# Load order, weight tiles and ReLU engines in a two-stage attention kernel with an MLP behind it

## The chip, the cores and the metric

One core of one Trainium2 chip runs the kernel. The metric is device microseconds of one execution.

## The reference

For 8 batches, 8 heads, 576 rows and head size 64, two softmax attentions follow one another, and an MLP with squared ReLU works on the result:

```python
def sm_attn(qq, kk, vv):
    s = scale * np.matmul(qq, kk.transpose(0, 1, 3, 2))
    s = s - np.max(s, axis=-1, keepdims=True)
    a = np.exp(s)
    a = a / (np.sum(a, axis=-1, keepdims=True) + 1e-09)
    return np.matmul(a, vv)
p_packed = sm_attn(p, k, v)            # p: 32 rows a head
attn = sm_attn(q, p_packed, p_packed)
x = attn.transpose(0, 2, 1, 3).reshape(4608, 512)
h = x @ w_in                           # 512 x 2048
r = np.maximum(h, 0.0)
out = (s * (r * r) + b) @ w_out        # 2048 x 512; s, b: one number each
```

Inputs and output are float32; the kernel computes in bf16 and accumulates in float32.

## The kernel before, in words

The unit of work is a batch (576 tokens). All matmuls are in one order written out by hand, as are the instructions of the other engines (`mm`, `tr` and the class `Pinned` keep program order, so L71, L74 and L82 are the lines of nearly every record). Steps of a batch `b`:

- `load` (line 93): q, k and v come by DMA issued on POOL, which also casts them to bf16; each has one buffer, so batch b+1's k waits for the last reader of batch b's. `load_p`, `load_w_in` (four chunks of 512 columns) and `load_w_out` (four chunks) use the same queue.
- `prep_p`, `prep_k`, `prep_q` (lines 194 to 254): transposes on PE, copies out of PSUM on DVE and ACT. From batch 3 on (`N_PE_T = 3`), `dma_k` and `dma_q` (lines 221, 256) transpose k and q by DMA from SP's queue instead, `dma_q` from a reordered copy that `order_q` makes on DVE; `order_v` makes another for v.
- `first_scores`, `packed`, `second_scores`, `weights` (lines 262 to 372): the two attentions, with exp on ACT, and ln and exp on ACT in place of a division; `weights` ends with the product `aT` on DVE.
- `packed_w` or `packed_w1` (lines 374, 399): the packed values times W_in, giving the batch's own weights `pw`; `packed_w1` does one chunk of 512 columns, with one half evicted by ACT and the other by DVE.
- `mlp_in(b, m)` (line 430), m from 0 to 15: four matmuls into a PSUM accumulator, a ReLU on ACT to `rlu` (three buffers), a square on DVE into `gT`.
- `Out.step` (line 471): the output tiles of 128 rows, each of 16 accumulating matmuls (steps) with `w_out_sb`; behind the last step DVE adds the bias row and SP stores the tile. `outs(b)` (line 498) gives four tiles for an even batch and five for an odd one; `run_outs(todo, n)` does n steps of them.
- `bias_part` (line 449): the sum of W_out's rows, once, in 16 matmuls.

PSUM holds three accumulators of two banks (pool `psh`, from `big()`) for everything but the output tiles, which have two of one bank (`psy`). `idle(n)` (line 167) is n matmuls on zeros.

The order: the loads are queued as batch 0, two chunks of W_in, batch 1, two chunks of W_in, W_out, p of batches 2 to 7. Lines 522 to 583 are a hand-made list: batch 0's attention, then its MLP inputs mixed with batch 1's attention, then the bias sum with the first output tile of batch 0 and MLP inputs of both batches. From line 585 on a loop over b runs the sixteen `mlp_in(b, m)`; between them stand the output steps of batch b-1 and, by `at(m, ...)`, the attention steps of batch a = b+1 and the loads and transposes of batch c = b+2.

Of the kernel before, what the change touches and what calls it, by code (L numbers as in the profile page):

```python
# [14 lines left out]
def kernel(  # L15
# [25 lines left out]
    P = 128  # L41
# [28 lines left out]
    def mm(*a, **kw):  # L70
        return tc.keep_in_program_order(nc.tensor.matmul(*a, **kw))  # L71
# [68 lines left out]
    bvec = constp.tile([P, 1], F32, name="bvec")  # L140
    sp.dma_start(out=bvec[:], in_=moe_b[0:1].unsqueeze(0).to_broadcast([P, 1]))
    nc.scalar.preload_act_table_set("natural_log_exp_and_others")
    load_w_in(0)
    load_w_in(1)

    KW = H * HS + 32
    kT = [constp.tile([P, KW], BF16, name=f"kT{i}") for i in range(2)]
# [46 lines left out]
    def prep_p(b):  # L194
        i = b % 2
        pt = big(BF16)
        for qd in range(NQ):
            tr(pt[:, 0, qd * P:(qd + 1) * P], pn[:, b, qd, :, :], identb[:])
        for c2 in range(2):
            vec.tensor_copy(  # L200
                out=pbd[i][D * c2:D * c2 + D, :, :, c2, :],
                in_=pt[D * c2:D * c2 + D, 0, 0:NQ * P].rearrange("p (q g j) -> p q g j", q=NQ, g=4),
            )

    def prep_k(b, half):

        i = b % 2
        tp = big(BF16)
        for h4 in range(4):
            for cp in range(CP):  # L210
                tr(
                    tp[:, h4 // 2, (h4 % 2) * HS + cp * R:(h4 % 2) * HS + (cp + 1) * R],
                    kn[b][:, 4 * half + h4, cp * P:(cp + 1) * P],
                    identb[0:R, 0:R],
                )
        vec.tensor_copy(
            out=kT[i][:, half * 4 * HS:(half + 1) * 4 * HS].rearrange("p (a s) -> p a s", a=2),
            in_=tp[:, :, 0:2 * HS],
        )
# [176 lines left out]
            else:  # L396
                vec.tensor_scalar_mul(out=dst, in0=tiles[qd][:], scalar1=rd[b][:, qd:qd + 1])

    def packed_w1(b, ch):

        i = b % 2
        if ch == 0:
            pw[b] = ppw.tile([P, NQ, DFF], BF16, tag="pw", name="pw")
        t = big()
        for qd in range(NQ):
            for pr in range(2):
                hp = 2 * qd + pr
                mm(
                    t[64 * pr:64 * pr + 64, qd, :],
                    ppbd[i][:, hp, :],  # L410
                    w_in_sb[:, hp, ch * NB:(ch + 1) * NB],
                    start=True,
                    stop=True,
                    tile_position=(0, 64 * pr),
                )
        dst = pw[b][:, :, ch * NB:(ch + 1) * NB]
        act.activation(out=dst[:, 0], in_=t[:, 0, :], func=AF.Copy, scale=rd[b][:, 0:1])
        vec.tensor_scalar_mul(out=dst[:, 1], in0=t[:, 1, :], scalar1=rd[b][:, 1:2])


# [6 lines left out]

        return 0 if (b % 4) in (1, 2) else NT * P

    def mlp_in(b, m):  # L430
        hps = big()
        for qd in range(NQ):
            for hf in range(2):
                mm(
                    hps[:, hf, 0:HS],
                    pw[b][:, qd, m * P:(m + 1) * P],
                    aT[b][:, qd, hf * HS:(hf + 1) * HS],
                    start=(qd == 0),
                    stop=(qd == NQ - 1),
                )  # L440
        rlu = ysp.tile([P, 2, HS], BF16, tag="rlu", name="rlu")
        act.activation(out=rlu[:], in_=hps[:, :, 0:HS], func=AF.Relu)
        g0 = slot(b) * S
        vec.tensor_tensor(
            out=gT[:, m, g0:g0 + S].rearrange("p (a s) -> p a s", a=2),
            in0=rlu[:], in1=rlu[:], op=ALU.mult,
        )

    def bias_part(cps, m):
        mm(cps[:], onesb[:], w_out_sb[:, m, :], start=(m == 0), stop=(m == NFF - 1))  # L450
        if m == NFF - 1:
            vec.tensor_scalar_mul(out=biasrep[:], in0=cps[:], scalar1=bvec[:])
# [63 lines left out]

    def loads(b):
        load(kn, k, b, "kn")
        load(vn, v, b, "vn")
        load(qn, q, b, "qn")  # L520

    idle(12)
    twice_p(0, 2)
    prep_k(0, 0)
    prep_p(0)
    first_scores(0, 0)
    prep_k(0, 1)
    first_scores(0, 1)
    prep_p(1)
    packed(0, 0)  # L530
    packed(0, 1)
    idle(3)
    prep_q(0, 0)
    prep_q(0, 1)
    second_scores(0)
    packed_w1(0, 0)
    weights(0, 0)
    weights(0, 1)
    packed_w1(0, 1)
    for m in range(0, 4):  # L540
        mlp_in(0, m)
    prep_k(1, 0)
    mlp_in(0, 4)
    prep_k(1, 1)
    first_scores(1, 0)
    mlp_in(0, 5)
    first_scores(1, 1)
    mlp_in(0, 6)
    packed(1, 0)
    packed(1, 1)  # L550
    mlp_in(0, 7)
    prep_q(1, 0)
    prep_q(1, 1)
    packed_w1(1, 0)
    second_scores(1)
    packed_w1(1, 1)
    weights(1, 0)
    packed_w1(0, 2)
    weights(1, 1)
    mlp_in(0, 8)  # L560
    mlp_in(0, 9)
    packed_w1(1, 2)
    mlp_in(0, 10)
    mlp_in(0, 11)
    packed_w1(0, 3)
    mlp_in(1, 0)
    mlp_in(1, 1)
    packed_w1(1, 3)
    mlp_in(0, 12)
    mlp_in(0, 13)  # L570
    loads(2)
    cps = psy.tile([P, NB], F32, tag="y", name="yps")
    todo = outs(0)
    rest = [(0, 14), (0, 15)] + [(1, m) for m in range(2, 7)]
    for m0 in range(0, NFF, 4):
        for m in range(m0, m0 + 4):
            bias_part(cps, m)
        for x in rest[0:1]:
            mlp_in(*x)
        run_outs(todo, 4)  # L580
        for x in rest[1:2]:
            mlp_in(*x)
        rest = rest[2:]

    for b in range(1, B):
        a = b + 1
        c = a + 1
        steps = {}

        def at(m, *fs):  # L590
            steps.setdefault(m, []).extend(fs)

        if b == 1:
            at(7, lambda: (twice_p(2, B), prep_p(2)))
            at(8, lambda: prep_k(2, 0))
            at(9, lambda: (prep_k(2, 1), first_scores(2, 0)))
            at(10, lambda: first_scores(2, 1))
            at(11, lambda: packed(2, 0))
            at(12, lambda: (packed(2, 1), prep_q(2, 0)))
            at(13, lambda: (prep_q(2, 1), packed_w(2, 0)))  # L600
            at(14, lambda: second_scores(2))
            at(15, lambda: weights(2, 0), lambda: weights(2, 1), lambda: packed_w(2, 1))
            at(10, lambda: loads(3))
            at(15, lambda: dma_k(3))
        elif a < B:
            d = 3 if b == 2 else 0
            at(0 + d, lambda: first_scores(a, 0))
            at(1 + d, lambda: first_scores(a, 1))
            at(3 + d, lambda: packed(a, 0))
            at(4 + d, lambda: packed(a, 1))  # L610
            at(6 + d, lambda: second_scores(a))
            at(8 + d, lambda: packed_w(a, 0))
            at(9 + d, lambda: weights(a, 0))
            at(10 + d, lambda: weights(a, 1))
            at(12 + d, lambda: packed_w(a, 1))
            if b == 2:
                at(1, lambda: (order_q(3), dma_q(3)))
                at(2, lambda: (prep_p(3), order_v(3)))
            if c < B:
                at(4, lambda: loads(c))  # L620
                at(13, lambda: (order_q(c), dma_k(c), dma_q(c)))
                at(15, lambda: (prep_p(c), order_v(c)))
        if b > 1:
            todo = outs(b - 1)
        per = 6 if b == 1 else len(todo)
        if b == 2:
            run_outs(todo, 8)
        for m in range(7 if b == 1 else 0, NFF):
# [9 lines left out]
_INS = ['q', 'k', 'v', 'p', 'moe_w_in', 'moe_w_out', 'moe_s', 'moe_b']  # L638
_OUTS = [((4608, 512), 'float32')]
# [25 lines left out]
```

## Time and profile before

| | |
|---|---|
| median of 3 runs | 286.64 us (286.24 to 288.02) |
| the profiled execution | 287.35 us, of which span 285.6 us |
| mean granted TensorE clock | 0.96 |
| PE busy | 259.3 us (91% of the span) |
| ACT, DVE, POOL busy | 145.8, 144.3, 27.7 us |
| DMA | 34.28 MB, mean 120 GB/s |

PE is the matmul engine (PEld its weight loads), DVE the vector engine, ACT the scalar engine, POOL GpSimd, SP the engine that issues stores and transposes. A record names output and inputs by the program's tile names: `yps` are output steps, `hps<-aT,pw` the matmuls of `mlp_in`, `hps<-w_in_sb,ppbd` those of `packed_w`. A granted clock of 1.00 is 2.4 GHz, 0.50 is 1.2 GHz. Matmuls are pipelined: a group's length holds a drain that the next group covers.

### The profile page before, as it was taken

The numbers are of one execution on the slowest core, as the hardware profiler recorded it, in microseconds if no ns is written. First come the engines' busy times: TensorE is split into PE (matmuls) and PEld (weight loads), VectorE is DVE, ScalarE is ACT, GpSimd is POOL, SyncE is SP. The second block draws the span as 40 slices with busy tenths as digits, with TensorE's granted clock in tenths as the row PEclk, the third lists the DMA queues.
The fourth block names the chain that finished last, engine by engine and source line by source line (L and its number), as shares of the span: only waits on it lengthen the run. The fifth ranks groups of instructions, "written<-read, shape, count | busy, mean of one in ns | idle before, by whom it ended". The sixth has DMA issues, their size and how long they took to land.

```text
span 285.6 us, 5198 instructions
## 1 busy us (share of the span) xinstructions
PE 259.3 (91%) x2127; PEld 145.7 (51%) x2127; DVE 144.3 (51%) x290; ACT 145.8 (51%) x219; POOL 27.7 (10%) x40
## 2 busy tenths in 40 slices
PE   8687869978999969889998999799989999999993
PEld 3544625545545634446555655465556555555441
DVE  3335567363548343735575447645674466444221
ACT  1257698424475434844765466346844674544000
POOL 8163200001201200030003000120000000000000
PEclk9757999999999988979999999999999999999998
DMA  7999999517495994799149951999192211121222
GB/s 86 193 205 205 206 204 198 83 37 115 71 192 80 151 197 82 140 159 221 45 81 154 223 109 37 171 166 204 35 182 67 55 39 38 54 59 37 73 73 73
DMA packets 54567, 34.28 MB, mean 120 GB/s; under 512 B 27408, under 2 KB 49936, under 8 KB 54544
## 3 DMA queue, kind: packets, MB, share of 16 engines
q0 software_dynamic: 25136, 18.61, 45.0%
q1 hardware_dynamic: 29408, 15.34, 25.6%
q8 instruction: 16, 0.26, 0.4%
q14 instruction: 7, 0.06, 0.1%
HBM read 37.23 MB, written 9.44 MB: 163 GB/s over the span
## 4 chain that ended last, share of the span: by engine, by line
PE 74%; DMA 10%; ACT 8%; DVE 5%; issue 1%; POOL 1%; POOLq 0%; DVEq 0%; ACTq 0%
PE yps L71 41%; PE hps L71 31%; DMA qT<-qr 5%; ACT rlu L82 3%; DMA vn<-in_v_dram 3%; DMA kT<-kn 2%; PE hps L74 2%; ACT rcd L82 1%; ACT ld L82 1%; ACT pw L82 1%; DVE gT L82 1%; DVE aT L82 1%; DVE kT L82 1%; DVE qr L82 1%; DVE pw L82 1%
## 5 line engine op out<-in xcount | busy, mean ns | idle before, releaser
L71 PE MATMUL yps<-w_out_sb,gT 128*128 128x512 bf16 x576 | 144.0, 383 | 0.0
L82 ACT ACTIVATE rlu<-hps 128x576 bf16<-128x576 f32 x128 | 82.8, 650 | 91.2 <-PE hps L71 84.3
L82 DVE TENSOR_TENSOR gT<-rlu 128x576 bf16<-128x576 bf16 x128 | 58.4, 457 | 94.2 <-ACT rlu L82 94.0
L71 PE MATMUL hps<-aT,pw 128*128 128x288 bf16 x512 | 85.1, 291 | 3.8 <-DVE aT L82 1.7
L71 PEld LDWEIGHTS <-gT 128*128 128x128 bf16 x576 | 53.2, 98 | 52.5 <-issue 7.5
L71 PEld LDWEIGHTS <-pw 128*128 128x128 bf16 x512 | 50.4, 100 | 41.0 <-issue 5.6
L82 DVE SCALAR_TENSOR_TENSOR ysb<-yps,svec,biasrep 128x512 f32<-128x512 f32 x36 | 26.9, 747 | 15.9 <-PE yps L71 15.8
L82 DVE TENSOR_SCALAR pw<-hps,rd 128x1024 bf16<-128x1024 f32 (+1 forms) x20 | 21.3, 1066 | 4.6 <-ACT pw L82 4.4
L82 ACT ACTIVATE e<-hps 96x768 bf16<-96x768 f32 x16 | 12.9, 804 | 16.4 <-PE hps L71 16.4
L82 POOL DMA_DIRECT2D kn<-in_k_dram x9 | 7.2, 799 | 130.9 <-DMA kT<-kn 84.3
L71 PE MATMUL hps<-w_in_sb,ppbd 128*64 128x512 bf16 x128 | 18.3, 392 | 1.7 <-ACT rlu L82 0.8
L82 ACT ACTIVATE pw<-hps,rd 128x1024 bf16<-128x1024 f32 (+1 forms) x20 | 18.8, 942 | 0.5 <-PE hps L71 0.3
L71 PE MATMUL hps<-pbd,kT 128*128 128x64 bf16 x192 | 9.3, 200 | 9.6 <-DVE pbd L82 3.4
L71 PEld LDWEIGHTS <-ppbd 128*64 128x64 bf16 x192 | 10.0, 113 | 14.0 <-issue 10.4
L82 DVE TENSOR_TENSOR aT<-e,rcd 128x576 bf16<-128x576 bf16 x16 | 12.1, 758 | 9.3 <-ACT rcd L82 9.2
L71 PEld LDWEIGHTS <-kT 128*128 128x128 bf16 x192 | 7.9, 102 | 12.2 <-DMA kT<-kn 4.3
L82 ACT ACTIVATE e<-hps,rs 128x576 bf16<-128x576 f32 x16 | 11.1, 740 | 2.8 <-PE hps L71 2.8
L82 ACT ACTIVATE rcd<-ld 128x576 f32<-128x576 f32 x16 | 10.9, 682 | 0.5
L82 ACT ACTIVATE ld<-hps 128x576 f32<-128x576 f32 x16 | 10.3, 642 | 0.0
L71 PE MATMUL hps<-qT,ppbd 128*64 128x288 bf16 x64 | 7.4, 328 | 2.8 <-DMA qT<-qr 2.3
L82 POOL DMA_DIRECT2D vn<-in_v_dram x8 | 6.2, 775 | 17.4 <-PE hps L71 13.8
L71 PE MATMUL hps<-zeros 128*128 128x512 bf16 x15 | 6.7, 629 | 1.3 <-DVE zeros L82 1.3
(46 smaller groups left out, 115.2 us busy)
## 6 DMA issues: line engine op xcount, KB each, us to landing
vn<-in_v_dram POOLq DMA_DIRECT2D x8, 576.0 KB, 11.2
qn<-in_q_dram POOLq DMA_DIRECT2D x8, 576.0 KB, 13.9
out_dram<-ysb SPq DMA_DIRECT2D x24, 192.0 KB, 2.8
kn<-in_k_dram POOLq DMA_DIRECT2D x7, 576.0 KB, 8.4
out_dram<-ysb SPq DMA_DIRECT2D x24, 128.0 KB, 2.4
w_in_sb<-in_moe_w_in_dram POOLq DMA_DIRECT2D x4, 512.0 KB, 14.3
w_out_sb<-in_moe_w_out_dram POOLq DMA_DIRECT2D x4, 512.0 KB, 20.0
out_dram<-ysb SPq DMA_DIRECT2D x24, 64.0 KB, 2.0
```

What stands on the lines that cost most here:

```text
L71: return tc.keep_in_program_order(nc.tensor.matmul(*a, **kw))
L74: return tc.keep_in_program_order(nc.tensor.transpose(*a, **kw))
L82: return lambda *a, **kw: tc.keep_in_program_order(f(*a, **kw))
```

## The change

All of W_in and W_out is queued behind batch 0 and ahead of batch 1. `mlp_in` and `packed_w1` get a switch `on_act`: with False, `mlp_in` does its ReLU on DVE and its square on POOL, and `packed_w1` evicts both halves on DVE. `m1` uses it for every third `mlp_in` of batches 0 and 1 (m = 2, 5, 8, 11, 14). The list is rewritten: batch 0 is carried through all its MLP inputs, the bias sum (now in an accumulator of `psh`) and two output tiles before batch 1's attention; the other two tiles (32 steps) stand between batch 1's attention steps; batch 1's sixteen `mlp_in` stand with batch 2's attention, and the loop starts with batch 2. Idle matmuls go from 15 to 30. In the loop, the loads, transposes and reorderings of batch c come at other steps, and q is loaded before v from batch 3 on.

```diff
     nc.scalar.preload_act_table_set("natural_log_exp_and_others")
-    load_w_in(0)
-    load_w_in(1)
+    for ch in range(NCH):
+        load_w_in(ch)
+    for m in range(0, NFF, 4):
+        load_w_out(m, m + 4)
...
     load(qn, q, 1, "qn")
-    load_w_in(2)
-    load_w_in(3)
-    for m in range(0, NFF, 4):
-        load_w_out(m, m + 4)
     load_p(2, B)
...
-        act.activation(out=dst[:, 0], in_=t[:, 0, :], func=AF.Copy, scale=rd[b][:, 0:1])
+        if on_act:
+            act.activation(out=dst[:, 0], in_=t[:, 0, :], func=AF.Copy, scale=rd[b][:, 0:1])
+        else:
+            vec.tensor_scalar_mul(out=dst[:, 0], in0=t[:, 0, :], scalar1=rd[b][:, 0:1])
...
-        act.activation(out=rlu[:], in_=hps[:, :, 0:HS], func=AF.Relu)
+        if on_act:
+            act.activation(out=rlu[:], in_=hps[:, :, 0:HS], func=AF.Relu)
+        else:
+            vec.tensor_scalar_max(out=rlu[:], in0=hps[:, :, 0:HS], scalar1=0.0)
         g0 = slot(b) * S
-        vec.tensor_tensor(
+        (vec if on_act else pool).tensor_tensor(
...
-        load(vn, v, b, "vn")
+        if b < N_PE_T:
+            load(vn, v, b, "vn")
         load(qn, q, b, "qn")
+        if b >= N_PE_T:
+            load(vn, v, b, "vn")
+
+    def m1(b, *ms):
+        for m in ms:
+            mlp_in(b, m, on_act=(m % 3 != 2))
```

The new list, in place of lines 522 to 583:

```python
idle(12); twice_p(0, 2)
prep_k(0, 0); prep_p(0); prep_k(0, 1); idle(3)
first_scores(0, 0); first_scores(0, 1); prep_p(1); idle(2)
packed(0, 0); packed(0, 1); idle(5)
prep_q(0, 0); prep_q(0, 1); idle(3)
second_scores(0); packed_w1(0, 0, on_act=False); idle(2)
weights(0, 0); weights(0, 1); idle(3)
packed_w1(0, 1, on_act=False); m1(0, 0, 1, 2, 3, 4)
packed_w1(0, 2, on_act=False); m1(0, 5, 6, 7, 8)
packed_w1(0, 3, on_act=False); m1(0, 9, 10, 11)
todo = outs(0); first, second = todo[0], todo[1]; bps = big()
for m0 in range(0, NFF, 4):
    for m in range(m0, m0 + 4):
        bias_part(bps[:, 0, :], m)
    if m0 < 8:
        m1(0, 12 + m0 // 2)
    first.step(4)
    if m0 < 8:
        m1(0, 13 + m0 // 2)
    second.step(4)
todo = todo[2:]
prep_k(1, 0); prep_k(1, 1); fill(4)      # fill(n): run_outs(todo, n)
first_scores(1, 0); fill(4); first_scores(1, 1); fill(4)
packed(1, 0); packed(1, 1); fill(4)
prep_q(1, 0); prep_q(1, 1); twice_p(2, B); fill(4)
packed_w1(1, 0); second_scores(1); fill(3)
packed_w1(1, 1); weights(1, 0); fill(3)
weights(1, 1); prep_p(2); fill(3)
packed_w1(1, 2); fill(3); loads(2); m1(1, 0, 1)
packed_w1(1, 3); m1(1, 2); prep_k(2, 0); m1(1, 3); prep_k(2, 1)
m1(1, 4, 5); first_scores(2, 0); m1(1, 6); first_scores(2, 1)
m1(1, 7, 8); packed(2, 0); m1(1, 9); packed(2, 1); m1(1, 10, 11)
prep_q(2, 0); prep_q(2, 1); m1(1, 12, 13); loads(3)
second_scores(2); m1(1, 14, 15); packed_w1(2, 0)
todo = outs(1); fill(6); weights(2, 0); fill(3)
packed_w1(2, 1); weights(2, 1); fill(6)
packed_w1(2, 2); fill(3); dma_k(3)
```

And the loop:

```diff
-    for b in range(1, B):
+    for b in range(2, B):
...
-        elif a < B:
-            d = 3 if b == 2 else 0
+        d = 3 if b == 2 else 0
+        if b == 2:
+            at(1, lambda: (packed_w1(2, 3), order_q(3), dma_q(3)))
+            at(2, lambda: (prep_p(3), order_v(3)))
+        if a < B:
             at(0 + d, lambda: first_scores(a, 0))
...
-            if c < B:
-                at(4, lambda: loads(c))
-                at(13, lambda: (order_q(c), dma_k(c), dma_q(c)))
-                at(15, lambda: (prep_p(c), order_v(c)))
+        if c < B:
+            at(1 + d, lambda: loads(c))
+            at(8 + d, lambda: dma_k(c))
+            at(10 + d, lambda: (order_q(c), dma_q(c)))
+            at(12 + d, lambda: order_v(c))
+            at(14, lambda: prep_p(c))
...
-        per = 6 if b == 1 else len(todo)
-        if b == 2:
-            run_outs(todo, 8)
-        for m in range(7 if b == 1 else 0, NFF):
+        per = len(todo)
+        for m in range(NFF):
             mlp_in(b, m)
```

## Rows read from the trace of the kernel before

**Rows 1.** Windows: PE, PEld, DVE, ACT, POOL busy (count), granted clock, DMA share, GB/s

```profile
27.50:48.00 20.50, 16.56 (x242) 10.31 (x240) 13.87 (x28) 17.11 (x29) 2.95 (x4) 1.00 1.33 203
...
92.00:110.00 18.00, 15.64 (x134) 9.01 (x135) 6.25 (x14) 7.32 (x12) 1.53 (x2) 0.91 1.25 173
...
118.00:127.00 9.00, 6.75 (x54) 3.58 (x52) 6.11 (x11) 4.45 (x7) 2.30 (x3) 0.81 1.00 159
...
150.00:153.00 3.00, 2.28 (x24) 1.25 (x22) 2.51 (x5) 1.59 (x3) 0.61 (x1) 1.00 0.97 135
...
180.00:186.00 6.00, 4.08 (x37) 2.44 (x36) 3.31 (x7) 2.11 (x3) 1.21 (x2) 1.00 1.06 177
...
213.00:285.60 72.60, 67.84 (x422) 36.23 (x420) 29.24 (x55) 26.85 (x41) 0.00 (x0) 0.98 0.23 59
```

**Rows 2.** PE's waits: who waited for whom, total us, times, longest

```profile
PE hps L71 <- DMA qT<-qr: 2.3, 1, 2.3
PE hps L71 <- DVE pbd L82: 2.2, 2, 1.7
...
PE hps L71 <- DMA kT<-kn: 1.9, 1, 1.9
```

**Rows 3.** Windows of two us, same columns

```profile
10.00:12.00 2.00, 1.10 (x16) 0.84 (x18) 0.85 (x3) 0.72 (x1) 0.66 (x1) 0.52 1.30 198
...
106.00:108.00 2.00, 2.00 (x12) 0.71 (x9) 0.00 (x0) 1.37 (x2) 0.00 (x0) 0.50 1.19 277
```

**Rows 4.** Timeline of PE: start, length, operation, count [idle before, releaser]

```profile
24.18 3.31 PE L71 MATMUL hps<-aT,pw 128*128 128x288 bf16 x14 [0.85 <-DVE aT L82]
...
85.86 0.87 PE L71 MATMUL hps<-aT,pw 128*128 128x288 bf16 x4
...
92.03 0.51 PE L71 MATMUL hps<-pbd,kT 128*128 128x64 bf16 x12 [0.47 <-DVE pbd L82]
...
106.74 2.31 PE L71 MATMUL yps<-w_out_sb,gT 128*128 128x512 bf16 x5
...
122.95 1.90 PE L71 MATMUL yps<-w_out_sb,gT 128*128 128x512 bf16 x4
```

**Rows 5.** Chain of waits (start, us, what), and one group of 27.5 to 48.0

```profile
46.14 1.71 PE hps L71 x12
...
49.20 0.86 PE yps L71 x4
50.55 0.86 PE yps L71 x4
...
L71 PE MATMUL hps<-aT,pw 128*128 128x288 bf16 x48 | 7.4, 287 | 1.4 <-ACT pw L82 0.9 <-DVE pw L82 0.5
```

**Rows 6.** Groups by form: busy us, mean ns | idle before, releasers

```profile
L82 ACT ACTIVATE rlu<-hps 128x576 bf16<-128x576 f32 x128 | 82.8, 650 | 91.2 <-PE hps L71 84.3 <-DVE rs L82 4.3 <-DVE rd L82 2.4
L82 DVE TENSOR_TENSOR gT<-rlu 128x576 bf16<-128x576 bf16 x128 | 58.4, 457 | 94.2 <-ACT rlu L82 94.0
...
L82 DVE TENSOR_SCALAR pw<-hps,rd 128x512 bf16<-128x512 f32 x8 | 6.0, 749 | 4.6 <-ACT pw L82 4.4
```

**Rows 7.** Timeline of the first 35 us: POOL's work and issues, one weight load

```profile
3.60 0.31 POOL L82 TENSOR_SCALAR_AFFINE_SELECT identb<-identb 128x128 bf16<-128x128 bf16 x1
...
21.09 0.11 PEld L71 LDWEIGHTS <-ppbd 128*64 128x64 bf16 x1 [0.59 <-DMA w_in_sb<-in_moe_w_in_dram]
...
24.15 0.75 POOL L82 DMA_DIRECT2D w_out_sb<-in_moe_w_out_dram  x1 [1.96 <-DMA kn<-in_k_dram]
...
30.27 0.78 POOL L82 DMA_DIRECT2D kn<-in_k_dram  x1 [2.14 <-DMA qn<-in_q_dram]
```

**Rows 8.** Timeline of SP's queue

```profile
122.42 1.41 SPq L82 DMA_DIRECT2D out_dram<-ysb  x2
```

**Rows 9.** Tiles kT and qT: DMA issue to landing, first kT's, then qT's

```profile
DMA to landing us min/median/max: 5.0/5.2/5.4
...
DMA to landing us min/median/max: 4.9/8.0/15.0
```

More of the change, by code (lines that the diff above doesn't have):

```diff
@@ L397, in packed_w, with packed_w1 @@
                 vec.tensor_scalar_mul(out=dst, in0=tiles[qd][:], scalar1=rd[b][:, qd:qd + 1])
-    def packed_w1(b, ch):
+    def packed_w1(b, ch, on_act=True):
         i = b % 2
@@ L428, in tail, with mlp_in @@
         return 0 if (b % 4) in (1, 2) else NT * P
-    def mlp_in(b, m):
+    def mlp_in(b, m, on_act=True):
         hps = big()
@@ L449, in bias_part @@
     def bias_part(cps, m):
-        mm(cps[:], onesb[:], w_out_sb[:, m, :], start=(m == 0), stop=(m == NFF - 1))
+        mm(cps, onesb[:], w_out_sb[:, m, :], start=(m == 0), stop=(m == NFF - 1))
         if m == NFF - 1:
-            vec.tensor_scalar_mul(out=biasrep[:], in0=cps[:], scalar1=bvec[:])
+            vec.tensor_scalar_mul(out=biasrep[:], in0=cps, scalar1=bvec[:])
     def store(ysb, i0, b, col, n):
@@ L525 @@
     prep_p(0)
+    prep_k(0, 1)
+    idle(3)
     first_scores(0, 0)
-    prep_k(0, 1)
     first_scores(0, 1)
     prep_p(1)
+    idle(2)
     packed(0, 0)
     packed(0, 1)
-    idle(3)
+    idle(5)
     prep_q(0, 0)
     prep_q(0, 1)
+    idle(3)
     second_scores(0)
-    packed_w1(0, 0)
+    packed_w1(0, 0, on_act=False)
+    idle(2)
     weights(0, 0)
     weights(0, 1)
-    packed_w1(0, 1)
-    for m in range(0, 4):
-        mlp_in(0, m)
+    idle(3)
+    packed_w1(0, 1, on_act=False)
+    m1(0, 0, 1, 2, 3, 4)
@@ new lines, with fill @@
+    packed_w1(0, 2, on_act=False)
+    m1(0, 5, 6, 7, 8)
+    packed_w1(0, 3, on_act=False)
+    m1(0, 9, 10, 11)
+    todo = outs(0)
+    first, second = todo[0], todo[1]
+    bps = big()
+    for m0 in range(0, NFF, 4):
+        for m in range(m0, m0 + 4):
+            bias_part(bps[:, 0, :], m)
[6 more added lines that the diff above has]
+    todo = todo[2:]
+    def fill(n):
+        run_outs(todo, n)
@@ L542 @@
     prep_k(1, 0)
-    mlp_in(0, 4)
     prep_k(1, 1)
+    fill(4)
     first_scores(1, 0)
-    mlp_in(0, 5)
+    fill(4)
     first_scores(1, 1)
-    mlp_in(0, 6)
+    fill(4)
     packed(1, 0)
     packed(1, 1)
-    mlp_in(0, 7)
+    fill(4)
     prep_q(1, 0)
     prep_q(1, 1)
+    twice_p(2, B)
+    fill(4)
     packed_w1(1, 0)
     second_scores(1)
+    fill(3)
     packed_w1(1, 1)
     weights(1, 0)
-    packed_w1(0, 2)
+    fill(3)
     weights(1, 1)
-    mlp_in(0, 8)
-    mlp_in(0, 9)
+    prep_p(2)
@@ L562 @@
+    fill(3)
     packed_w1(1, 2)
[L563 to L567, printed above, removed]
-    packed_w1(1, 3)
[L569 to L583, printed above, removed]
@@ L585 @@
-    for b in range(1, B):
+    fill(3)
+    loads(2)
+    m1(1, 0, 1)
+    packed_w1(1, 3)
+    m1(1, 2)
+    prep_k(2, 0)
+    m1(1, 3)
+    prep_k(2, 1)
+    m1(1, 4, 5)
+    first_scores(2, 0)
+    m1(1, 6)
+    first_scores(2, 1)
+    m1(1, 7, 8)
+    packed(2, 0)
+    m1(1, 9)
+    packed(2, 1)
+    m1(1, 10, 11)
+    prep_q(2, 0)
+    prep_q(2, 1)
+    m1(1, 12, 13)
+    loads(3)
+    second_scores(2)
+    m1(1, 14, 15)
+    packed_w1(2, 0)
+    todo = outs(1)
+    fill(6)
+    weights(2, 0)
@@ L586 @@
+    fill(3)
+    packed_w1(2, 1)
+    weights(2, 1)
+    fill(6)
+    packed_w1(2, 2)
+    fill(3)
+    dma_k(3)
+    for b in range(2, B):
         a = b + 1
@@ L591, in at @@
             steps.setdefault(m, []).extend(fs)
[L593 to L604, printed above, removed]
-        elif a < B:
-            d = 3 if b == 2 else 0
+        d = 3 if b == 2 else 0
[3 more added lines that the diff above has]
+        if a < B:
             at(0 + d, lambda: first_scores(a, 0))
@@ L615 @@
             at(12 + d, lambda: packed_w(a, 1))
-            if b == 2:
-                at(1, lambda: (order_q(3), dma_q(3)))
-                at(2, lambda: (prep_p(3), order_v(3)))
-            if c < B:
-                at(4, lambda: loads(c))
-                at(13, lambda: (order_q(c), dma_k(c), dma_q(c)))
-                at(15, lambda: (prep_p(c), order_v(c)))
-        if b > 1:
+        if c < B:
[4 more added lines that the diff above has]
+            at(14, lambda: prep_p(c))
+        if b > 2:
             todo = outs(b - 1)
-        per = 6 if b == 1 else len(todo)
-        if b == 2:
-            run_outs(todo, 8)
-        for m in range(7 if b == 1 else 0, NFF):
+        per = len(todo)
+        for m in range(NFF):
             mlp_in(b, m)
@@ L631 @@
                 f()
-            run_outs(todo, per)
-        run_outs(todo, NFF * (NT + 1))
+            fill(per)
+        fill(NFF * (NT + 1))
     todo = outs(B - 1)
     while todo:
-        run_outs(todo, NFF)
+        fill(NFF)
 _INS = ['q', 'k', 'v', 'p', 'moe_w_in', 'moe_w_out', 'moe_s', 'moe_b']
```

## The prediction

> **What bounds the kernel now.** I read the windows by stage first, then PE's waits with their releasers, then fine windows for the clock, and last the rows of single engines and queues. In the windows [rows 1] the reader is to see three regimes. From 27.5 to 48.0 us PE is busy 16.56 of 20.5: batch 1's attention steps and batch 0's MLP inputs run with no output tiles between them, and ACT (17.11) and DVE (13.87) empty accumulators about as fast as PE fills them. Late in the kernel PE is full: 67.84 of the last 72.60, the rest being the tail after the last matmul. Between lie holes: 2.36 us in 92 to 110, 2.25 in 118 to 127, 0.72 in 150 to 153 and the same again in 210 to 213, 1.92 in 180 to 186. Their releasers are the transposed queries, pbd's copies waiting in a full DVE queue, and kT arriving late [rows 2]. Behind the first two holes PE also runs at 1.2 GHz for a while: the granted clock is 0.50 in 106 to 108 [rows 3], five output steps took 2.31 us and, behind the second, four took 1.90 [rows 4], where 0.215 each and a drain of 0.17 make 1.24 and 1.03. That is some 1.2 us beyond each of the two.
>
> **The sum** is made against the profiled execution (287.35 us; span 285.6, so 1.75 outside it), which lies 0.71 above the median 286.64 of the runs; a saving is taken off either. PE's prices at 2.4 GHz: four output steps are 0.86 us in a period of 1.35 that also holds one mlp_in, so an output step is 0.215 and an mlp_in 0.49 [rows 5]. Twelve matmuls in 1.71 us hold a packed_w1 and two mlp_in; without those and the drain a packed_w1 is 0.55 [rows 5]. A batch's attention steps: 16.56 less the twelve mlp_in there (48 matmuls [rows 5]) and six packed_w1 leaves 7.4, of which I take off 1.4 for eleven drains that the next group covers: 6.0. Other engines [rows 6]: ReLU on ACT 0.65, square on DVE 0.457, half of a packed_w1 on DVE 0.749. The ReLU on DVE has no row; 576 columns for 512 make 0.84 of the last, between 0.65 (ACT's) and twice that.
>
> **1. The loads.** W_in 2 and 3 and W_out move ahead of batch 1 on POOL's queue. W_in 1 landed when its matmul was released, at 21.05 us; POOL's sixteenth issue was held until 24.15, when the eighth (batch 1's k) landed, the eighteenth until 30.27, when the tenth landed [rows 7]. So at most eight are under way, they land in order, and 576 KB take 3.07 us, 512 KB 2.73. Forward from 21.05: W_in 2 23.8, W_in 3 26.5, W_out 29.3 to 37.4, batch 1's k 40.5, v 43.6, q 46.6. POOL is held until the ninth lands (26.5) and then issues p, so its first square begins at 27.5.
>
> **2. Start to the first mlp_in.** It hangs on the landings of v, q and W_in 0, which stay. The change adds fifteen idle matmuls, 3.9 us at 2.4 GHz, in waits for those landings. If they keep the clock up (before, it fell to 0.52 in 10 to 12, with PE busy 1.10 of 2 us [rows 3]), second scores end 1 us earlier and the chain of exp, ln, exp and product brings the first mlp_in at 23.2 instead of 24.2 [rows 4]: plus 1.0. If not, the idles cost 7.7 us at 1.2 GHz, of which about 3 fall behind the landings: minus 2.
>
> **3. First mlp_in to batch 2's loop.** Batch 0's first twelve mlp_in with three packed_w1, both halves now on DVE: 6 x 0.749, 4 ReLUs x 0.84, 8 squares x 0.457 = 11.5 us on DVE against 7.0 on PE. PE is let on when the third accumulator from the end is empty: 10.6 us, to 33.9. Bias sum and two output tiles: 48 x 0.215 + 4 x 0.49 = 12.3, to 46.1; the last W_out is wanted at 43.5 and q of batch 1 at 53, each some 6 us after landing, so the new order of the loads costs nothing. Batch 1's attention with 32 output steps: 6.0 + 6.9 + 3 x 0.55 + 0.15 for prep_p = 14.7; walking the list with three accumulators adds 1.8, mostly ACT's exp, ln, exp. 16.5, to 62.6. Then batch 1's sixteen mlp_in with batch 2's attention, and no output step between them, since batch 1's tiles need the last square: 7.8 + 0.55 + 5.5 = 13.9 on PE; the walk adds 3.7, to 80.2 (at the 81% that PE was busy from 27.5 to 48.0 it would be 17.2 for my 17.6). Three packed_w1, weights and 18 steps: 6.0 + 0.4, to 86.6. Bounds: with no wait 80.7, with all waits doubled 92. Before, the loop began at 85.9 [rows 4] with eight output steps done instead of 18 and one packed_w1 more: 10 x 0.215 - 0.55 = 1.6, so 87.4 for the same work. **The start gains about 0.8 (bounds +6.7 and -5).**
>
> Squares on POOL (ten): POOL has no two-input row. Bounds 0.46 (DVE's own) and 2.8 (twice 576/128 of the affine select's 0.313 [rows 7]); I take the single 1.4. Its buffer is wanted again three mlp_in later, 1.7 us at least, so nothing is paid; at 2.8 some 0.5 each, 5 us in all at worst. The Trainium skill (GPSIMD Engine Reference, Elementwise side-by-side cycle accounting) gives about 2.6 cycles an element for two inputs; by it a square is an estimated 1.25 us and the sum stays. No row here shows it.
>
> **4. kT of batch 3.** dma_k(3) stands behind the stores of batch 1's first output tile in SP's queue. That tile's sixteenth step is in the last fill before the loop; DVE has aT, half a packed_w1 and the tile's own sum before the stores: 88.4. Two stores took 1.41 [rows 8]; the transpose goes out at 89.8 and lands 5.2 later [rows 9], at 95.0. PE comes to first_scores(3, 0) at 91.8. **A new wait of 3.2 us**, with all of PE's queue behind it, and 1.2 of half clock as behind the old holes. Before, the step began at 92.0 [rows 4] with 23 output steps done; now 30. Behind by (95.0 - 92.0) - 7 x 0.215 + 1.2 = 2.7, the start's gain included. Bounds: no wait at all (1.7 ahead), or 15.0 [rows 9] instead of 5.2.
>
> **5. What the earlier transposes remove.** dma_q(3) now leaves ahead of batch 4's loads and is wanted some ten us later: its hole and slow stretch go, 2.36 + 1.2 = 3.6. dma_k, order_v and prep_p of the batches behind come one to five steps earlier: 2.25 + 1.2, less 0.5 for a pw buffer that stays late, = 2.9; and 0.72 + 1.92 + 0.72 = 3.4. A step is at least 1.35 us: two earlier cover 2.7, five 6.7. Next late would be DVE, where order_v now meets packed_w; I bound that with 0.5 in each of four batches. Loads, transposes and stores are issued as often as before.
>
> **Sum:** 3.6 + 2.9 + 3.4 - 2.7 = 7.2. 287.35 - 7.2 = 280.15; from the median, 286.64 - 7.2 = **279.4 us**.
>
> **The rivals.** (a) *No new wait, and the accumulators hold less*: kT lands in time (4.4) and half of the 6 us of walked waits isn't there (3): 272.0. For it: PE is full wherever output steps are mixed in; against it: 27.5 to 48.0.
> (b) *The start gives back what the later part wins*: the clock stays low behind the sparse beginning (-3) and half of the waits double (-3): 285.4. For it: 0.52 in 10 to 12; against it: 1.00 in the whole of 27.5 to 48.0 [rows 1].
> (c) *Slower: kT(3) collides with loads(3).* The transpose of qT that ran beside batch 4's loads took 15.0 us, the quickest 4.9 [rows 9]. If loads(3) still run when dma_k(3) goes out, it lands 9.8 later: 289.2. I have them issued at 76 to 78 and through by 87 (three of 3.07 and some 2 to begin), 2.8 before the transpose; that margin decides. The Trainium skill (DMA: Bandwidth & Descriptors, Queues, rings and completion order) says that a DMA engine takes turns between its queues, packet by packet. By that rule any overlap stretches kT in proportion; the trace's 15.0 agrees.
> (d) *The clock falls between 62 and 80*, where PE is 79% busy with short matmuls: 13.9 us at half speed add up to 9. If half of the stretch is slow the end is 284, if all of it 288.4.
>
> **How the numbers follow.** A measurement here tells about 1% (2.9 us) from no change. My forecast (276 to 283.7): 0.50. (a) and what lies beyond: 0.17. (b) and the milder (d), 283.8 to 289: 0.21. (c), or (d) with some of (b): 0.12. Faster 0.66, same 0.21, slower 0.13. The range goes from (a) to just past (b), 272 to 286, and leaves out some 0.07 below and 0.13 above.
>
> **What would show it.** Steps 1 and 3: W_out landing from 29 to 37 us, bias matmuls from 34 on, batch 2's first mlp_in near 86.6, PE 63 to 80% busy in 23 to 34 and 62 to 80. Step 4: PE waiting for kT between 91 and 95; if it doesn't, (a). Step 5: no hole of PE of 0.7 us or more behind 100 us but the tail. Squares on POOL of about 1.4 us that hold nobody. I am wrong if the holes behind 100 us stay, if the granted clock is 0.5 in any stretch from 28 to 90, or if batch 2's loop begins outside 81 to 92.

## The result, and the profile after

The change ran in 279.29 us (median of four runs, 277.73 to 285.89) against 287.02 for the kernel before beside it: ratio 0.9711, 95% interval 0.9654 to 0.9768. Here and below, a ratio leaves out runs more than 1.5% above the fastest of the same kernel, such as this 285.89, while a median is of all runs. The forecast was 279.4 from the median, 280.15 for the profiled execution. That took 279.46 (span 277.6), 7.89 less than the 287.35 of before.

Windows of the kernel after (us; busy us and count of PE, PEld, DVE, ACT, POOL; granted clock, DMA share, GB/s):

```profile
24.50:35.60 11.10, 7.71 (x54) 4.60 (x54) 9.97 (x17) 4.99 (x8) 4.60 (x4) 1.00 1.25 206
35.60:48.00 12.40, 12.40 (x67) 6.31 (x66) 4.56 (x8) 1.95 (x3) 2.29 (x2) 1.00 1.03 137
...
63.70:81.10 17.40, 15.08 (x230) 10.32 (x230) 14.15 (x28) 10.73 (x17) 6.83 (x7) 1.00 0.13 25
...
92.00:100.00 8.00, 5.30 (x42) 2.98 (x41) 3.70 (x8) 3.04 (x5) 2.35 (x3) 0.79 0.96 159
...
119.00:128.00 9.00, 9.00 (x105) 5.84 (x104) 6.51 (x13) 5.09 (x8) 1.31 (x2) 1.00 1.36 166
...
180.00:186.00 6.00, 6.00 (x67) 3.93 (x66) 3.07 (x7) 2.74 (x5) 0.00 (x0) 1.00 0.97 200
```

They answer to [rows 1]. PE is full where the holes were (119 to 128, 180 to 186). One hole is new, in 92 to 100. In the first 11.1 us behind the first full `mlp_in` (the point from which PE has both halves of `aT`; two matmuls stand alone a little ahead of it), PE works 7.71 and DVE 9.97: the stretch goes at DVE's pace. From 63.7 to 81.1 the clock stays at 1.00.

PE's waits after, which answer to [rows 2]:

```profile
PE hps L71 <- DMA kT<-kn: 2.7, 1, 2.7
PE hps L71 <- DVE pw L82: 2.5, 3, 1.4
...
PE hps L71 <- DMA qT<-qr: 0.3, 1, 0.3
```

And the timeline of PE after at the points that the prediction named (start, length, operation, count, wait before it); it answers to [rows 4]:

```profile
24.52 0.90 PE L71 MATMUL hps<-aT,pw 128*128 128x288 bf16 x6 [0.83 <-DVE aT L82]
...
35.64 1.03 PE L71 MATMUL hps<-w_out_sb,onesb 128*128 128x512 bf16 x4
...
87.38 0.66 PE L71 MATMUL hps<-aT,pw 128*128 128x288 bf16 x4
...
95.56 0.53 PE L71 MATMUL hps<-pbd,kT 128*128 128x64 bf16 x12 [2.70 <-DMA kT<-kn]
...
130.29 0.68 PE L71 MATMUL hps<-qT,ppbd 128*64 128x288 bf16 x8 [0.32 <-DMA qT<-qr]
```

Batch 2's loop begins at 87.38; before, the same work stood at 87.4 by the prediction's working. So the new start gains nothing, and all of the 7.89 us comes behind it. In five other traces with this start (runs 2, 3, 5, 6 and 9) the loop begins at 88.43 to 89.05, so that there it loses 1.0 to 1.6. The wait for batch 3's kT is there, 2.70 us where 3.2 was forecast.

### The profile page after: what moved, and what is told of

It is laid out like the page before. It is cut to its first block, busy times and chain, and to the rows that moved or that the text cites. A ratio compares the mean times of both kernels' runs of the same rounds, so it can differ in the third digit from the quotient of the medians.

```text
span 277.6 us, 5233 instructions
## 1 busy us (share of the span) xinstructions
PE 257.6 (93%) x2142; PEld 143.5 (52%) x2142; DVE 151.1 (54%) x296; ACT 137.2 (49%) x207; POOL 39.4 (14%) x50
## 4 chain that ended last, share of the span: by engine, by line
PE 77%; DMA 9%; DVE 6%; ACT 5%; issue 2%; POOL 1%; POOLq 0%; DVEq 0%; ACTq 0%
PE yps L71 42%; PE hps L71 32%; DMA qT<-qr 4%; DMA vn<-in_v_dram 3%; PE hps L74 2%; DMA kT<-kn 2%; DVE gT L82 2%; ACT rlu L82 2%; DVE pw L82 1%; ACT rcd L82 1%; ACT ld L82 1%; ACT e L82 1%; POOL kn L82 1%; DVE rlu L82 1%; DVE ysb L82 1%
## 5 line engine op out<-in xcount | busy, mean ns | idle before, releaser
L82 ACT ACTIVATE rlu<-hps 128x576 bf16<-128x576 f32 x118 | 76.4, 649 | 84.2 <-PE hps L71 74.9
L82 DVE TENSOR_TENSOR gT<-rlu 128x576 bf16<-128x576 bf16 x118 | 56.1, 479 | 70.3 <-ACT rlu L82 69.5
L71 PE MATMUL hps<-aT,pw 128*128 128x288 bf16 x512 | 83.3, 288 | 5.2 <-DVE pw L82 2.5
L71 PEld LDWEIGHTS <-pw 128*128 128x128 bf16 x512 | 49.3, 98 | 40.7 <-issue 6.3
L82 DVE TENSOR_SCALAR pw<-hps,rd 128x512 bf16<-128x512 f32 (+1 forms) x26 | 24.4, 950 | 3.4 <-ACT pw L82 2.1
L82 ACT ACTIVATE pw<-hps,rd 128x1024 bf16<-128x1024 f32 (+1 forms) x18 | 16.6, 922 | 1.1 <-PE hps L71 1.1
L82 POOL TENSOR_TENSOR gT<-rlu 128x576 bf16<-128x576 bf16 x10 | 11.6, 1162 | 27.9 <-DVE rlu L82 27.9
L71 PEld LDWEIGHTS <-ppbd 128*64 128x64 bf16 x192 | 8.9, 109 | 11.7 <-issue 7.8
L71 PE MATMUL hps<-zeros 128*128 128x512 bf16 x30 | 9.8, 465 | 2.2 <-DVE zeros L82 1.3
L82 ACT COPY qT<-hps 128x576 bf16<-128x576 bf16 x6 | 3.6, 640 | 10.1 <-PE hps L74 10.1
```

The costliest lines, as they stand in the source:

```text
L82: return lambda *a, **kw: tc.keep_in_program_order(f(*a, **kw))
```

## The experiments

Short names: the **start** is all up to batch 2's loop, the **loop** the rest. Each ratio is to the kernel before, run beside it.

**1. The loop's steps alone.** The kernel before, with its loads, list and engines, and only this:

```diff
-                at(4, lambda: loads(c))
-                at(13, lambda: (order_q(c), dma_k(c), dma_q(c)))
-                at(15, lambda: (prep_p(c), order_v(c)))
+                at(1 + d, lambda: loads(c))
+                at(8 + d, lambda: dma_k(c))
+                at(10 + d, lambda: (order_q(c), dma_q(c)))
+                at(12 + d, lambda: order_v(c))
+                at(14, lambda: prep_p(c))
```

and q loaded before v from batch 4 on.

> The kernel before with one part of the change alone: in the loop, the loads, transposes and reorderings of batches 4 to 7 at the change's steps, q loaded before v there. The list up to batch 2 and the load order of the weights stay old. Theory (the loop's earlier transposes bring the gain): the holes at 118 to 127, 150, 180 and 210 us go, 2.9 + 3.4 = 6.3 us, the hole near 104 us stays: about 280.7, ratio 0.978. Rival (the new list and load order bring it): about 287, ratio 1.00, and the holes were only hidden idle time.

Measured: 278.99 us, ratio 0.9753 [0.9661, 0.9846]. The wait for batch 3's qT stays, and the windows behind it are full (of 9, 3 and 6 us, PE had 6.75, 2.28 and 4.08 before [rows 1]). Timeline and windows of this run:

```profile
106.80 0.68 PE L71 MATMUL hps<-qT,ppbd 128*64 128x288 bf16 x8 [3.40 <-DMA qT<-qr]
```
```profile
118.00:127.00 9.00, 8.37 (x91) 5.34 (x93) 6.95 (x13) 5.66 (x8) 1.54 (x2) 1.00 0.95 111
150.00:153.00 3.00, 3.00 (x34) 1.98 (x34) 0.80 (x2) 1.51 (x3) 0.00 (x0) 1.00 1.39 153
180.00:186.00 6.00, 5.89 (x66) 3.93 (x66) 3.17 (x8) 2.59 (x4) 0.00 (x0) 1.00 1.18 229
```

Five lines of schedule bring as much as the whole change.

**2. The rest alone.** The kernel after, with the loop's old five lines put back.

> The kernel after with that part undone: batches 4 to 7 loaded, transposed and reordered at the old steps of the loop, v before q; the new list and the new load order stay. Theory: the 6.3 us come back, 279.3 + 6.3 = 285.6, ratio to before 0.995, and the start alone is worth next to nothing. Rival: the start holds the gain, about 279 to 281, ratio 0.975.

Measured: 285.57 us (ten runs, 285.1 to 286.91), ratio 1.0019 [0.9988, 1.0051]. PE's waits of this run:

```profile
PE hps L71 <- DMA kT<-kn: 6.3, 4, 2.7
```

Three waits for kT are back beside the new one of 2.7. Loads, list, ReLUs and idles together are worth nothing that can be measured: the two medians (285.57 and 287.97) would make it 0.992, some 2.4 us at most.

**3. Batch 3's kT early.** The kernel after, with k of batch 3 loaded and transposed during batch 1's MLP inputs:

```diff
     prep_k(2, 1)
+    load(kn, k, 3, "kn")
...
     m1(1, 10, 11)
+    dma_k(3)
...
-    loads(3)
+    load(qn, q, 3, "qn")
+    load(vn, v, 3, "vn")
...
-    dma_k(3)
```

> The kernel after, with k of batch 3 loaded as soon as batch 2's k is transposed, and transposed by DMA ahead of batch 1's output stores instead of behind the first of them. Theory: PE's wait of 2.7 us for kT at 93 to 95.6 and the half clock behind it (about 1.2) go: 3.9 us, about 275.4, ratio to before 0.960. Rival: what is late next (pbd's copies or the transposed q on DVE and SP) takes its place within the same steps: less than 1.5 us, 278 or more.

Measured: 281.84 us (279.22 to 283.56), ratio 0.9802 [0.9687, 0.9917]. The wait for kT went, and two for qT came:

```profile
PE hps L71 <- DMA qT<-qr: 2.4, 2, 1.4
```

The loop took 188.45 us in its profiled execution, against 190.22 after: 1.8 of the 3.9 expected is kept, and 2.4 goes into waits for qT. The one of 0.95 us is for batch 3's q. POOL's issue of batch 4's k and SP's transpose of batch 3's q, in this run and then after:

```profile
84.22 0.83 POOL L82 DMA_DIRECT2D kn<-in_k_dram  x1
94.14 3.10 SPq L82 DMA_TRANSPOSE qT<-qr  x1
```
```profile
93.60 2.96 SPq L82 DMA_TRANSPOSE qT<-qr  x1
96.55 0.82 POOL L82 DMA_DIRECT2D kn<-in_k_dram  x1 [13.94 <-issue]
```

After, k's one buffer is held until batch 3's kT has landed (PE's wait for it ends at 95.56), so batch 4's k leaves behind the transpose of q. With kT early it leaves ahead of that transpose, and q of batch 4, at 94.29, runs beside it.

**4. The old order of the loads under the new list.** W_in 2 and 3 and W_out go back behind batch 1's q.

> The kernel after with the old load order alone: batch 1 ahead of the second half of W_in and of W_out. Theory (the new list needs the new order): W_in 2 lands at 33 instead of 24 us and the last W_out at 46 instead of 37; the list wants them at 27.5 and 45.4, so PE waits some 5 us for W_in 2 and the rest follows: 284 to 285, ratio 0.991. Rival (the order of the loads makes no difference, the transfers are hidden either way): 279, ratio 0.973.

Measured: 289.72 us, ratio 1.0012 [0.9937, 1.0088]. PE's waits:

```profile
PE hps L71 <- DMA qT<-qr: 5.0, 2, 4.5
PE hps L71 <- DMA w_in_sb<-in_moe_w_in_dram: 4.2, 1, 4.2
```

The third chunk of W_in is late by 4.2 us: from the first full `mlp_in` to the bias sum it is 15.7 us (25.70 to 41.40) for 11.1 after. So the list needs this order. The rest beyond what was expected goes with the long wait for qT, which is not the edit's doing: runs 6 to 8 show one of 2.7 to 4.5 us without the edit.

**5. The change once more.**

> The kernel after, unchanged, to stand beside the next kernels on the same chip: both theories expect 279 to 280, ratio to before about 0.975.

Measured: 284.48 us (280.53, 284.25, 284.72, 286.28), ratio 0.9826 [0.9731, 0.9922]. The profiled one (280.53) has its first full `mlp_in` at 25.87, 1.35 later than above, and no wait for qT. So the change's own time moves between 277.7 and 286.3 from run to run, and it was to be found out by what.

**6. Loads of the next batch placed at the end of the batch before** (with 3's early kT):

```diff
-            at(1 + d, lambda: loads(c))
+            if b == 2:
+                at(4, lambda: loads(4))
+            if c + 1 < B:
+                at(15, lambda: loads(c + 1))
```

> The kernel after with the early kT of batch 3, and with the loads of batches 5 to 7 moved on to the end of the batch ahead of the one that transposes them (batch 4's leave at step 4 as before), so that no transpose of q runs beside loads. Theory (the gain of the early kT was given back because the q transposes landed late beside loads): q lands in about 5 us, the waits for it (0.95 and 1.4 us) go, and the loop comes out 3.5 to 4 us shorter than the kernel after: about 275.5. Rival (DVE's copies are late next, whatever the transposes do): 277 or more.

Measured: 279.67 us (277.21, 277.53, 281.81, 282.26), ratio 0.9625 [0.9544, 0.9706], which is of the two runs of 277 alone; the medians make it 0.973. The theory on placing fell: in the profiled execution (281.81) the loads had not moved; those of 277 were not traced. The timeline of this run, POOL's issue of k of batch 5, SP's transpose of q of batch 4, and PE:

```profile
114.11 0.77 POOL L82 DMA_DIRECT2D kn<-in_k_dram  x1 [17.63 <-DMA kT<-kn]
...
116.87 3.59 SPq L82 DMA_TRANSPOSE qT<-qr  x1
...
131.13 0.88 PE L71 MATMUL hps<-qT,ppbd 128*64 128x288 bf16 x8 [2.91 <-DMA qT<-qr]
```

After, the same issue stands at 115.20 with the same releaser: k has one buffer, so k of batch 5 leaves the moment batch 4's kT has landed, wherever the list has it. That load, with q's behind it, then runs beside the transpose of q, and PE waits 2.91 us.

**7. No square on POOL.** The ReLUs stay split; all squares on DVE:

```diff
-        (vec if on_act else pool).tensor_tensor(
+        vec.tensor_tensor(
```

> The kernel after with the ten squares of POOL given to DVE; the ten ReLUs stay on DVE. Theory (POOL's squares hold up DVE's squares while they run): DVE's squares are all 0.46 us again, none over 0.5, against a mean of 0.62 and single ones of 1.17 to 1.34 where POOL works; DVE pays ten more squares (4.6 us) and saves about 2.6, so the two stretches with the split (24.5 to 35.6 and 63.7 to 81.1) are longer by 1 us each at most, total 279.3 to 281. Rival (the long squares come from somewhere else): they stay long, and the stretches grow by 2 us each, 283.

Measured: 281.46 us (279.32 to 285.34), ratio 0.9742 [0.9649, 0.9836]: the qT wait (4.45 us in its profiled execution) hides the effect in the runs' times, so it is read from the start, whose clock is 1.00 in both. From the first full `mlp_in` to the loop it takes 88.04 - 27.48 = 60.6 us; after, 87.38 - 24.52 = 62.9. All eight traces with the split and POOL's squares that keep the order of the loads (the change and runs 2, 3, 5, 6, 8, 9, 10) have 62.9, with the first full `mlp_in` anywhere from 24.52 to 26.19. The theory had expected this stretch to grow. Its first stretch and that of after (24.50:35.60, above):

```profile
27.40:36.80 9.40, 7.68 (x54) 4.62 (x54) 9.26 (x19) 5.00 (x8) 0.27 (x1) 1.00 1.25 206
```

DVE does POOL's squares as well and PE reaches the bias sum 1.7 us earlier. The tile gT of the kernel after shows why (ns, min/median/max, first and last start), with one pair of its timeline:

```profile
L82 DVE TENSOR_TENSOR gT<-rlu x118: 441/459/1336, 25.7 to 255.8; 128x576 bf16<-128x576 bf16 x118
L82 POOL TENSOR_TENSOR gT<-rlu x10: 1146/1147/1291, 27.4 to 81.5; 128x576 bf16<-128x576 bf16 x10
```
```profile
74.25 1.15 POOL L82 TENSOR_TENSOR gT<-rlu 128x576 bf16<-128x576 bf16 x1 [2.13 <-DVE rlu L82]
...
74.55 1.17 DVE L82 TENSOR_TENSOR gT<-rlu 128x576 bf16<-128x576 bf16 x1 [0.37 <-ACT rlu L82]
```

A square on DVE that meets one on POOL takes 1.17 us, elsewhere up to 1.34, in place of 0.46; POOL's stay at 1.147, with 1.29 the longest. Without POOL (this run) the longest of 128 is 460 ns.

**8. Fifteen idle matmuls, as before the change** (12 at the beginning and 3 ahead of `prep_q(0, 0)`).

> The kernel after with the fifteen added idle matmuls taken out again (12 and 3 as before, no others). Theory (landings and ACT's chain set the first mlp_in): the first full mlp_in at 24 to 25.5 us as with them, total within 1 us of the kernel after. Rival (they hold the clock): granted clock 0.5 from 10 to 20 us and on into the first mlp_in, first mlp_in at 26 or later, total 281.5 or more.

Measured: 283.42 us, ratio 0.9843 [0.9787, 0.9899], with a wait of 2.7 for qT. Timeline and window of this run, and the window of run 5 behind it:

```profile
24.53 0.90 PE L71 MATMUL hps<-aT,pw 128*128 128x288 bf16 x6 [0.85 <-DVE aT L82]
```
```profile
10.00:20.00 10.00, 9.31 (x158) 6.93 (x157) 3.17 (x9) 3.53 (x5) 3.02 (x4) 0.51 1.28 206
```
```profile
10.00:20.00 10.00, 8.80 (x156) 5.99 (x159) 3.29 (x11) 2.63 (x4) 2.84 (x5) 0.72 1.28 206
```

The clock is lower with fewer idles (0.51 for 0.72), and yet the first full `mlp_in` comes 1.3 us earlier than in run 5 (24.53 for 25.87). Against the first trace of the change, with thirty idles, 0.83 in this window and 24.52, it comes at the same time. So the added idles gain nothing here. That they cost something isn't shown: the three traces with fifteen and this list (runs 8, 10, 12) have 24.53 to 25.16, eight of the nine with thirty 25.57 to 27.48, but PE starts on the second half of batch 0's k at 9.77 to 9.88 in the three and at 10.58 to 10.84 in the eight (8.62 in the first trace), and up to there the two lists are alike. What sets that time is open.

**9. q's transpose ahead of k's.** The kernel after, with:

```diff
-            at(8 + d, lambda: dma_k(c))
-            at(10 + d, lambda: (order_q(c), dma_q(c)))
+            at(9 if b == 2 else 7, lambda: (order_q(c), dma_q(c)))
+            at(10 if b == 2 else 8, lambda: dma_k(c))
```

So k's buffer, and with it the next load, comes free only when q's transpose is under way.

> The kernel after with one pair in the loop turned round: q of batch c is reordered and transposed first (step 7, step 9 for batch 4), k one step behind it. POOL's next loads begin with k and so are held until both transposes are out. Theory (the loads of batch 5 start as soon as kT of batch 4 has landed, whatever their place in the list, and slow the transpose of q that follows): q of batch 4 lands in 5 to 6 us instead of 10 to 16, no wait for it near 130 us (0.3 to 4.5 us so far), and all runs lie near the fast ones of the kernel after, 279 to 281. Rival (the slower runs have another cause): runs at 284 to 286 stay, the median with them.

Measured: 280.14 us (six runs, 278.44 to 282.21), ratio 0.9745 [0.9696, 0.9794]. PE has no wait for qT. Issue to landing of qT, here and then in the kernel after:

```profile
DMA to landing us min/median/max: 4.8/5.1/6.4
```
```profile
DMA to landing us min/median/max: 4.8/10.6/16.6
```

Runs of 283 to 286 are gone. That speaks for the collision as their cause: in the traced runs 7 and 11 it held PE for 4.45 and 4.59 us. The long runs of the change itself were not traced, and the change was not run beside this kernel.

**10. The mendings together.** Runs 3, 8 and 9 in one, and `mlp_in(2, 3)` with its ReLU on DVE and its square on POOL, behind which the loads of batch 4 wait.

> Everything that the runs so far favour, on the kernel after: k of batch 3 loaded and transposed early, q ahead of k in the loop, the fifteen added idle matmuls out, and the square of batch 2's fourth mlp_in on POOL so that batch 4's loads stay behind q of batch 3. Theory: no wait of PE for a transpose at all, 2.8 + 1.2 for kT and 0.3 to 4 for q, about 275.5, ratio to before 0.958, better than both kernels. Rival (DVE or the accumulators are late next): 279 or more.

Measured: 277.16 us (six runs, 276.56 to 277.5), ratio 0.9614 [0.9582, 0.9646]. The one wait for a DMA transpose is 0.8 us; 24.64 to 87.58, the stretch of run 7, is still 62.9. The time is 1.7 over the theory's, well under the rival's.

**11. All ReLUs on ACT, all squares on DVE.** The kernel after, with:

```diff
-            mlp_in(b, m, on_act=(m % 3 != 2))
+            mlp_in(b, m)
```

> The kernel after with every ReLU on ACT and every square on DVE (packed_w1 of batch 0 stays on DVE). Theory (the split is worth its place): in the stretch of batch 1's sixteen mlp_in, 17.4 us long, ACT's sum goes from 10.7 to 14.0 us plus its waits, so it is 1 to 2 us longer, total 280.5 to 281.5. Rival (POOL's squares cost DVE what ACT saves): within 0.5 us of the kernel after in that stretch, total 279 to 280.

Measured: 280.46 us (277.27 to 282.87), ratio 0.9682 [0.9619, 0.9745], with 4.59 us of wait for qT in the profiled execution. Its timeline and first stretch:

```profile
26.16 0.90 PE L71 MATMUL hps<-aT,pw 128*128 128x288 bf16 x6 [0.83 <-DVE aT L82]
...
34.44 1.02 PE L71 MATMUL hps<-w_out_sb,onesb 128*128 128x512 bf16 x3
...
85.14 0.65 PE L71 MATMUL hps<-aT,pw 128*128 128x288 bf16 x4
```
```profile
26.10:34.40 8.30, 7.49 (x54) 4.50 (x54) 7.63 (x16) 6.50 (x11) 1.02 (x1) 1.00 1.24 207
```

The stretch takes 59.0 us, 3.9 less than after. Both the theory and the rival were off on it: 2.8 of the 3.9 lie ahead of the bias sum and 1.0 behind it. With run 7, one execution of each: the ten ReLUs on DVE cost 60.6 - 59.0 = 1.6 in all, the ten squares on POOL another 2.3. The 11.1 us to the bias sum become 8.3, in which PE is 90% busy.

**12. Run 10 with all ReLUs of batches 0 and 1 on ACT.** Run 10 is the base meant in the expectation.

> The kernel of the ninth experiment but one (fifteen idle matmuls, k of batch 3 early, q's transpose ahead of k's, one gate on POOL) with all ReLUs of batches 0 and 1 on ACT and their squares on DVE; the gate at mlp_in(2, 3) stays. Theory: the split of the ReLUs costs 3.9 us between the first full mlp_in and batch 2's loop (62.9 us with it, 59.0 without, each in one execution), and nothing that I mended elsewhere gives it back. Then that stretch is 59.0 long, the loop behind it 187.5 as with the split, and the time about 273.3 us, ratio 0.948. Rival: what the list saves is waited for at the loop, because the transposed k of batch 3 and the loads of batch 4 keep their times: a new wait for kT or qT of 2 us or more in the loop, and 275.5 us or more, ratio 0.956 or above.

Measured: 273.24 us (six runs, 271.95 to 274.55), ratio 0.9532 [0.9476, 0.9587], faster than both kernels. Its timeline and first stretch:

```profile
25.16 0.90 PE L71 MATMUL hps<-aT,pw 128*128 128x288 bf16 x6 [0.85 <-DVE aT L82]
...
85.76 0.65 PE L71 MATMUL hps<-aT,pw 128*128 128x288 bf16 x4
```
```profile
24.50:35.00 10.50, 9.10 (x54) 5.08 (x54) 8.35 (x16) 6.71 (x11) 1.27 (x2) 0.84 1.24 206
```

The stretch is 60.6 long, 1.6 over the forecast, since the clock was not yet up behind 25 us (0.84 in the window); the loop is 271.7 - 85.76 = 185.9 for 187.5, and PE has no wait for a DMA transpose. The two misses cancel in the time. Against run 10 the medians give 3.9 us and the ratios 0.8%, some 2.3 us, each against the before beside it: whole runs put the split's cost between 2.3 and 3.9.

## Why the prediction was right, and where it was not

**The sum and its main terms stand.** The gain comes from step 5, the earlier transposes: run 1 has it without the rest, run 2 the rest without it. Holes behind 100 us are gone but for the tail, 0.32 and 0.19 us. Step 4's new wait came at its place and nearly its size: 2.70 us for 3.2, the half clock behind it (window of the kernel after):

```profile
97.00:99.00 2.00, 2.00 (x18) 1.40 (x17) 0.30 (x1) 0.64 (x1) 1.90 (x3) 0.50 0.83 106
```

Run 3 shows that taking it away alone returns 1.8, because the waits for qT were next, which the prediction did not ask. One of them undoes the first term of step 5. `dma_q(3)` stands at batch 2's step 1 and `loads(4)` at its step 4 in both kernels; before, k of batch 4 left at 89.68, ahead of the transpose of q at 90.52, and after it left behind it only since the late kT held k's buffer (run 3). So the 2.70 paid and the 3.6 gained hang on one event, and rival (a), which kept the gain and took the wait away, could not come whole with this list. Run 10 has both, by a gate that holds the loads.

**Step 3** placed the bias sum at 33.9 (35.64 measured), the end of batch 1's MLP inputs at 80.2 (81.12) and the loop at 86.6 (87.38): right in kind, DVE's pace first and PE's second, 0.8 late at the end. W_out and batch 1 landed in time, as step 1 had it. So the start gained 0 in place of 0.8, and the loop 7.9 in place of 6.4. Of that 1.5, the 0.5 set down for a pw buffer was not needed (119 to 128 is full). A good part of the rest is the half clock, set down at 1.2 each time. Second scores of batch 3, first scores of batches 4 and 5, before and then after:

```profile
105.64 1.17 PE L71 MATMUL hps<-qT,ppbd 128*64 128x288 bf16 x8 [2.33 <-DMA qT<-qr]
...
122.49 0.65 PE L71 MATMUL hps<-pbd,kT 128*128 128x64 bf16 x12 [1.69 <-DVE pbd L82]
...
151.88 0.52 PE L71 MATMUL hps<-pbd,kT 128*128 128x64 bf16 x12 [0.72 <-ACT rlu L82]
```
```profile
107.14 0.68 PE L71 MATMUL hps<-qT,ppbd 128*64 128x288 bf16 x8
...
119.97 0.51 PE L71 MATMUL hps<-pbd,kT 128*128 128x64 bf16 x12
...
147.23 0.51 PE L71 MATMUL hps<-pbd,kT 128*128 128x64 bf16 x12
```

Between these points PE does the same work in both, but for one output step in the first stretch. Less that step and PE's waits there (1.69 and 0.56, then 0.72 before; 0.19, then 0.32 after) the old kernel took 1.75 us longer in the first and 1.73 in the second, and that is what half clock behind the two holes cost. Step 4's own cost 1.65: from the end of the wait for kT to batch 3's second scores it is 11.58 us after, and 9.93 in run 9, which has the same wait and a clock of 1.00.

**Where it failed.** (i) "Nothing is paid" for squares on POOL: right on the buffer, with 1.147 us for the 1.4 taken, but the price is on DVE, which was the bound there. It is 2.3 us, inside the 5 that stood as worst case, and for a reason not named. The ReLU on DVE, at 0.752 us, was cheaper than the 0.84 taken, and still the ten cost 1.6. (The 7.0 us of PE set beside DVE's 11.5 are 7.5 by the prediction's own prices; nothing hung on it.) The Trainium skill (GPSIMD Engine Reference, 8. Key points) says that GpSimd shares its SBUF interfaces with VectorE and contends with VectorE instructions that have two SBUF inputs; the squares are such, and the 1.17 us pair agrees. (ii) Step 2's "plus 1.0" for idles: 24.52 for 23.2, and 25.57 or later in the other traces with thirty. The choice of 1.0 rested on the clock, and in run 8 the first full `mlp_in` comes at 24.53 with the clock at 0.51. The other end, minus 2, is nearer to most traces; whether the idles are its cause is open (run 8). (iii) Step 5 counted "five earlier cover 6.7" for q's transpose too. It now runs beside batch 5's loads: 0.32 us of wait in the trace of the change, up to 4.59 in traces of kernels with the same loop. That is rival (c)'s mechanism, one batch later and one tensor on; the prediction had it, at k of batch 3 only.

These errors nearly cancel in the profiled execution; that 279.4 came so near to 279.29 is in part luck. Rivals (b) and (d) did not come: the clock was 1.00 from 24.5 to 87.4. Nor did (c) where it was placed: kT of batch 3 went out at 90.21 and PE was let on at 95.56. Of (a) nothing came.

## What to carry to other kernels

Split a change by where it stands in time: five lines of schedule held the gain, and the rest, though it moved every load and half the list, was worth nothing that can be measured, in good part because ReLUs and squares moved off ACT cost 2.3 to 3.9 us. Move work to an engine only where that engine has time in that stretch: DVE was the bound in 24.5 to 35.6, and ACT had half of it free. With one buffer, a load goes out when its last reader is done, not where the list puts it; the order of the readers is what moves it.

## What the runs showed of the hardware

- Squares of 128x576 bf16 on DVE and on POOL at the same time: DVE's took up to 1.34 us for 0.46, POOL's stayed at 1.147, with 1.29 the longest of ten.
- The granted clock of 10 to 20 us was 0.51 to 0.83 in nine traces with thirty idle matmuls and 0.50 to 0.52 in three with fifteen (runs 8, 10, 12). At 0.51 the first full `mlp_in` came at 27.48 with thirty (run 7) and at 24.53 with fifteen (run 8); at 0.83 it came at 24.52 (the change) and 25.57 (run 9).
- Behind one and the same wait of PE, 2.68 to 2.80 us for batch 3's kT, the clock fell to 0.50 in four traces (the change, runs 2, 5, 8) and stayed at 1.00 in four (runs 4, 7, 9, 11). From that wait to second scores it was 11.45 to 11.59 us in the first four and 9.92 to 9.93 in the others.
- A transpose by DMA that lands 4.8 us after its issue at the quickest took 16.6 at the longest in the same trace. What PE then waited for batch 4's q was 0 and 0.32 us in two traces of the change, and 4.45 and 4.59 in two kernels with the same loop (runs 7 and 11).
